# A spectral layer and a gated SwiGLU on one core: the D transform first, gate and up over both token groups, h times w2 in seven products, the sequence transform last

## The chip, the core and the metric

The kernel runs on one core of a Trainium2 chip. The metric is the time of one execution on the device, in microseconds (us); the median of three runs of the kernel before is 728.52 us (728.14 to 728.65). Engines in the text: TensorE (PE; its weight loads are PEld), VectorE (DVE), ScalarE (ACT), GpSimd (POOL, used here to start DMAs) and SyncE (SP, which starts most DMAs). On-chip memory is SBUF; matmul results go to PSUM, eight banks of 128 x 512 float32.

## The reference

For x of 2048 tokens by 512 features (S x D), in float32:

```
a = x @ hid_re.T ;  b = x @ hid_im.T            # transform along D
y = seq_re @ a - seq_im @ b                     # transform along S, real part
h = silu(x @ w1) * (x @ w3)                     # 1376 hidden features (F)
o = h @ w2
g = sigmoid((x * gate_w).sum(-1))
out = g * y + (1 - g) * o
```

## The kernel before

**Precision.** Each operand of a matmul is split into a high part, a copy rounded to the matmul's float32r format, and a low part, the difference (`split`, L75 to L77: a ScalarE copy, then a VectorE subtraction). `mm3` (L79 to L81) then issues three matmuls, high x high, high x low, low x high. So each product costs three 128x512 matmuls, and each operand one ACT and one DVE pass.

**Seven products.** A 2 x 2 block product is done with seven block products instead of eight (Strassen's scheme in Winograd's form). Sums of blocks of each operand are made first (the "forms" T1 to T4 on one side, `forms`, L95, on the other), and the seven results, P1 to P7, are added up out of PSUM. Gate and up, the sequence transform and the D transform are done this way; h times w2 is a plain product.

**Stages**, in this order:

1. Gate and up for token group 0 (1024 tokens). F is cut into 11 chunks of 128 (NC); w1 and w3 of a chunk and the two halves of D make the 2 x 2 blocks. The first chunk is done plainly, in eight products (`plain`, L340). `gate_up` (L308) runs over the others with `first1`, `first2` and `second`: 42 matmuls each. `prep_wa` and `prep_wb` make the weights' forms, three chunks ahead (LOOK). The gate score is the last column block of w1 (`put_score`).
2. `down` (L269) for group 0: h times w2, 264 matmuls into eight banks. The split w2 is also written to DRAM (`w2sp`).
3. Gate and up and `down` for group 1; w2 is read back from `w2sp`. Beside it `prep_d` (L110) makes the forms of the D matrices and writes them to DRAM (`dsp`), and `load_a` makes the forms of x for the sequence transform.
4. The sequence transform on x, four blocks of 512 transform rows (1344 matmuls `P<-zo,a`): `CHAIN` (L472) lists the seven products, `step` (L590) issues one of them, with four pieces (q) per product. `advance` (L534) runs ahead of it: loads eight steps ahead (`load_c`, LEAD + AHEAD), sums four ahead (`sum_c`), splits three ahead (`split_c`, L513). After the split of B22 a POOL DMA adds B12 to it in place (`accum_op`, L522). `spill` scales by the gate and writes to DRAM (`zsp`).
5. The D transform on these results, two blocks (336 matmuls `P<-zo,d`), reading `zsp`, then the closing sum with (1 - g) o from `nbsp`, and the output.

**What sets the order.** Each engine runs its instructions in the order of the built program; a scheduler lays that out beforehand from the dependencies, so it stays near the source order but not equal to it. The DMA queues of SP and POOL are in order too: a DMA that waits holds up those behind it. Most 4 KB-per-partition tiles come from one pool (`f4`, 13 buffers); a tile waits until the last user of its buffer is done, a store's landing included.

Of the kernel before, what the change touches and what calls it, by code (L numbers as in the profile page):

```python
# [12 lines left out]
P = 128  # L13
S = 2048
D = 512
F = 1376
KD = D // P
TB = 512
NTB = S // TB
NT = TB // P  # L20
NST = S // P
NG = NST // 2
NC = (F + P - 1) // P
NC2 = (NC + 1) // 2
WARM = 11
# [3 lines left out]
def fnet_swiglu_gate_kernel(  # L29
    ctx: ExitStack,  # L30
    tc: tile.TileContext,
    xn: bass.AP,
# [4 lines left out]
    w2: bass.AP,  # L37
    out: bass.AP,
# [6 lines left out]

    nc = tc.nc

    def pool(name, bufs, side, space=None):
        kw = {} if space is None else {"space": space}
        cm = tc.tile_pool(name=name, bufs=bufs, side=side, reuse_waits="tile", **kw)
        return cm, cm.__enter__()

    def close(*cms):
        for cm in reversed(cms):
            cm.__exit__(None, None, None)
# [4 lines left out]
    f4 = ctx.enter_context(tc.tile_pool(name="f4", bufs=13, side="right"))  # L63
    dn_cm, dn = pool("dn", 2, "right")
    xo_cm, xo = pool("xo", 1, "left")
    wo_cm, wo = pool("wo", 2, "left")
    tp_cm, tp = pool("tp", 2, "left")

    def bank(k, name):
        return psum.tile([P, 512], F32, tag=f"ps{k}", name=name)  # L70

    def wide(name):
        return f4.tile([P, 1024], F32, tag="f4", name=name)

    def split(hi, lo, src):  # L75
        nc.scalar.activation(hi, src, AF.Copy)  # L76
        nc.vector.tensor_sub(lo, src, hi.bitcast(F32))  # L77

# [4 lines left out]

    act0 = const.tile([P, 1], F32, tag="act0", name="act0")
    nbsp = dram.tile([D, S], F32, tag="nbsp", name="nbsp")
    gs = dram.tile([NTB, 1, 512], F32, tag="gs", name="gs")
    gsp = dram.tile([2, P, 1024], F32, tag="gsp", name="gsp")
    dsp = [dram.tile([KD, P, 2, n, 256], F32, tag=f"dsp{n}", name=f"dsp{n}") for n in (4, 3)]
    w2sp = dram.tile([NC, P, 2, 512], F32, tag="w2sp", name="w2sp")
    zsp = dram.tile([4 * NTB * P, 1024], F32, tag="zsp", name="zsp")  # L90

    def flat(ap):
        return ap.rearrange("p a n -> p (a n)")

    def forms(r, m, t1, t2):  # L95

        r, m = (v.rearrange("p (a n) -> p a n", a=4) for v in (r, m))
        a21, a11, a12, a22 = (r[:, i] for i in range(4))  # L100
        nc.vector.tensor_sub(m[:, 0], a22, a21)  # L101
        for d, v, w in ((1, m[:, 0], a11), (2, a12, m[:, 1])):
            nc.vector.scalar_tensor_tensor(m[:, d], v, -1.0, w, op0=ALU.mult, op1=ALU.subtract)  # L103
        nc.vector.tensor_sub(m[:, 3], a11, a21)  # L104
        split(t1[:, 0, 0], t1[:, 1, 0], a11)
        split(flat(t1[:, 0, 1:4]), flat(t1[:, 1, 1:4]), flat(m[:, 0:3]))
        split(flat(t2[:, 0, 0:2]), flat(t2[:, 1, 0:2]), flat(r[:, 2:4]))
        split(t2[:, 0, 2], t2[:, 1, 2], m[:, 3])

    def prep_d(p):  # L110

        r, m = wide(f"dr{p}"), wide(f"dm{p}")
        t1 = dn.tile([P, 2, 4, 256], F32R, tag="ho", name=f"d1_{p}")
        t2 = dn.tile([P, 2, 4, 256], F32R, tag="ho", name=f"d2_{p}")[:, :, :3]
        nc.sync.dma_start(r, dd[p])
        forms(r, m, t1, t2)
        nc.sync.dma_start(dsp[0][p], t1.bitcast(F32))
        nc.sync.dma_start(dsp[1][p], t2.bitcast(F32))


    XO, ST = {}, {}
    XRAW = ("B12", "B11", "B21", "B22")

    def flat_x(ap):
        return ap.rearrange("p q n -> p (q n)")

    def load_xo(g, k):

        if g not in XO:
            XO[g] = xo.tile([P, 2, 7, 2, 512], F32R, tag="xo", name=f"xo{g}")  # L130
        ST[g, k] = wide(f"xs{g}_{k}")
        nc.sync.dma_start(ST[g, k], xt[g, XRAW.index(k)])

    OPS = ("B11", "B21", "B22", "T1", "T2", "T3", "T4")
    SUMS = {"T1": ("B12", "B11"), "T2": ("B22", "T1"), "T3": ("B22", "B12"), "T4": ("B21", "T2")}

    def sum_xo(g, k):
        ST[g, k] = wide(f"xs{g}_{k}")
        nc.vector.tensor_sub(ST[g, k], *(ST[g, v] for v in SUMS[k]))

    def split_xo(g, k):
        o = XO[g][:, :, OPS.index(k)]
        split(flat_x(o[:, 0]), flat_x(o[:, 1]), ST[g, k])

    WS, WA, WB = {}, {}, {}
    LOOK = 3

    def load_w(i, lo=0, hi=4, queue=nc.sync):
        if lo == 0:
            WS[i] = wo.tile([P, 4, 256], F32, tag="ws", name=f"ws{i}", bufs=LOOK + 1)  # L150
        queue.dma_start(WS[i][:, lo:hi].rearrange("p a n -> p (a n)"),
                          w13[i % NC, :, lo * 256 : hi * 256])

    def prep_wa(i, lo=0, hi=3):

        if lo == 0:
            WA[i] = wo.tile([P, 2, 3, 256], F32R, tag="wa", name=f"wa{i}", bufs=LOOK + 1)
        t = WA[i]
        split(t[:, 0, lo:hi].rearrange("p a n -> p (a n)"),
              t[:, 1, lo:hi].rearrange("p a n -> p (a n)"),  # L160
              WS[i][:, lo:hi].rearrange("p a n -> p (a n)"))

    def prep_wb(i, part=None):

        if part != 1:
            w = WS.pop(i)
            u = wo.tile([P, 4, 256], F32, tag="wu", name=f"wu{i}", bufs=1)
            nc.vector.tensor_add(u[:, 0], w[:, 3], w[:, 2])
            nc.vector.tensor_sub(u[:, 1], u[:, 0], w[:, 0])
            nc.vector.tensor_sub(u[:, 2], w[:, 0], w[:, 3])  # L170
            nc.vector.tensor_sub(u[:, 3], w[:, 1], u[:, 1])
            WB[i] = u
        if part != 0:
            u = WB[i]
            t = wo.tile([P, 2, 4, 256], F32R, tag="wb", name=f"wb{i}")
            split(t[:, 0].rearrange("p a n -> p (a n)"), t[:, 1].rearrange("p a n -> p (a n)"),
                  u.rearrange("p a n -> p (a n)"))
            WB[i] = t

    def prod(ps, i, wi, xi, start, chain=False):  # L180
        g = i // NC
        w, wi = (WA[i], wi) if wi < 3 else (WB[i], wi - 3)
        x = XO[g]
        for q in range(2):
            sl = slice(q * P, (q + 1) * P)
            mm3(ps, w[:, 0, wi, sl], w[:, 1, wi, sl], x[:, 0, xi, q, :], x[:, 1, xi, q, :],
                start and q == 0, q == 1, chain)

    G, H = {}, {}

    def first1(i):
        x = bank(i % 4, f"X{i}")
        prod(x, i, 0, 0, True)
        s1 = tp.tile([P, 512], F32, tag="s1", name=f"s1_{i}", bufs=LOOK + 2)
        nc.scalar.activation(s1, x, AF.Copy)
        G[i] = (x, s1)

    def first2(i):

        y = bank(4 + i % 2, f"Y{i}")  # L200
        prod(y, i, 1, 1, True)
        s1 = G[i][1]
        nc.vector.tensor_add(s1, s1, y)
        put_score(i, 0, s1)
        nc.scalar.activation(s1, s1, AF.Silu)

    SC = {}

    def put_score(i, j, gate):


        if i % NC < NC - 1:
            return
        if j == 0:
            SC[i] = tp.tile([P, 2, 512], F32, tag="sc", name=f"sc{i}", bufs=1)
        nc.scalar.activation(SC[i][F % P :, j], gate[F % P :], AF.Copy)
        if j == 1:
            nc.sync.dma_start(gs[2 * (i // NC) : 2 * (i // NC) + 2].rearrange("b o n -> o b n"),
                              SC[i][F % P : F % P + 1])

    def second(i, between):
        x, s1 = G.pop(i)
        z = bank(6 + i % 2, f"Z{i}")
        u2 = tp.tile([P, 512], F32, tag="u2", name=f"u2_{i}")
        u4 = tp.tile([P, 512], F32, tag="u4", name=f"u4_{i}")
        g1 = tp.tile([P, 512], F32, tag="g1", name=f"g1_{i}")
        h = wide(f"h{i}")
        H[i] = h
        prod(x, i, 4, 4, False, True)
        nc.scalar.activation(u2, x, AF.Copy)  # L230
        prod(z, i, 5, 5, True, True)
        nc.scalar.activation(u4, z, AF.Copy)
        between[0]()
        prod(x, i, 3, 3, False, True)
        nc.vector.tensor_add(u4, u4, x)
        prod(z, i, 2, 6, False, True)
        nc.vector.tensor_add(u2, u2, z)
        nc.vector.tensor_mul(h[:, :512], s1, u2)
        between[1]()
        prod(x, i, 6, 2, False, True)  # L240
        put_score(i, 1, x)
        nc.scalar.activation(g1, x, AF.Silu)
        nc.vector.tensor_mul(h[:, 512:], g1, u4)

    HO, W2R, W2O = {}, {}, {}

    def load_w2(i):
# [21 lines left out]
    def down(g, extra):  # L269
# [4 lines left out]
        for c in range(NC):  # L274
            if c == 0:
                load_w2(g * NC + 1)
# [444 lines left out]
```

## Time and profile before

| | |
|---|---|
| median of three runs | 728.52 us |
| the profiled execution, first to last instruction (span) | 728.3 us |
| instructions | 8383 |
| matmuls | 3149, 11 of them warm-up |
| moved by DMA | 132.41 MB, 182 GB/s on average |
| mean granted TensorE clock | 0.996 |

The runs' times and the span differ by about 0.2 us, so a span can be read as a time. In the profile a line of a group gives the source line, engine, operation, output<-input, shape and count, then the busy time in us and the mean of one instruction in ns, then the idle time of that engine just before and what ended it. Because `split` and `mm3` are helpers, groups are told apart by their tiles.

### The profile page before, as it was taken

The page shows a single profiled execution, that of the slowest core. Times are in us where ns is not written, and L with a number is a line of the kernel's source. Part 1 is how long each engine was busy: PE and PEld are TensorE (multiplying, and loading weights), DVE is VectorE, ACT ScalarE, POOL GpSimd, SP SyncE. Part 2 cuts the span into 40 slices and gives each one's busy share as a digit, 9 for nine tenths or more (in the row PEclk, how much of TensorE's full clock was granted, in tenths as well). Part 3 has the DMA queues.
Part 4 walks back from the last instruction along what each step waited for, and adds up shares of the span by engine and source line. Part 5 has one row for each costly group of instructions (what it writes and reads, how often), then busy time and mean ns, then how long its engine had stood idle before and what let it go on. Part 6 is the DMA issues. An engine that isn't in the chain of part 4 may idle for free.

```text
span 728.3 us, 8383 instructions
## 1 busy us (share of the span) xinstructions
PE 720.7 (99%) x3149; PEld 590.7 (81%) x3149; DVE 542.9 (75%) x677; ACT 358.5 (49%) x458; POOL 21.3 (3%) x28
## 2 busy tenths in 40 slices
PE   9999999999999999998999999999999999999997
PEld 6888878888888888877888888888888888888886
DVE  6987786574598974799867786687758785667875
ACT  6655555454475743565444444444444444445451
POOL 0000000000000000000010001000000001000000
PEclk9999999999999999999999999999999999999999
DMA  6112135833157503585957733874195719999942
GB/s 259 59 58 87 58 118 200 291 128 145 37 188 279 191 1 99 182 328 196 377 95 240 257 120 64 243 246 155 29 234 185 253 23 218 366 380 305 332 161 86
DMA packets 37772, 132.41 MB, mean 182 GB/s; under 512 B 3938, under 2 KB 4322, under 8 KB 36708
## 3 DMA queue, kind: packets, MB, share of 16 engines
q1 hardware_dynamic: 33988, 118.90, 45.6%
q0 software_dynamic: 3456, 12.58, 9.5%
q8 instruction: 24, 0.39, 0.2%
q10 hardware_dynamic: 288, 0.39, 0.1%
q14 instruction: 16, 0.13, 0.1%
HBM read 100.93 MB, written 30.94 MB: 181 GB/s over the span
## 4 chain that ended last, share of the span: by engine, by line
PE 93%; DVE 3%; DMA 2%; ACT 1%; issue 1%; SPq 0%; DVEq 0%; ACTq 0%
PE P L81 52%; PE X L81 15%; PE acc L81 12%; PE Z L81 8%; PE Y L81 4%; PE C L81 2%; DVE a L77 1%; DMA w2o<-w2sp 1%; DMA xr<-xn 1%; DMA xs_B<-xt 1%; DVE xm L103 0%; DVE xm L101 0%; DVE xm L104 0%; ACT L303 0%; DVE ho L77 0%
## 5 line engine op out<-in xcount | busy, mean ns | idle before, releaser
L81 PE MATMUL P<-zo,a 128*128 128x512 f32 x1344 | 304.8, 389 | 0.0
L81 PEld LDWEIGHTS P<-zo,a 128*128 128x128 f32 x1344 | 252.3, 188 | 52.4
L76 ACT ACTIVATE zo<-B 128x1024 fp32r<-128x1024 f32 x124 | 131.4, 1060 | 159.9 <-PE P L81 148.4
L77 DVE TENSOR_TENSOR zo<-B,zo 128x1024 fp32r<-128x1024 f32 x124 | 151.5, 1223 | 76.5 <-ACT zo L76 76.1
L81 PE MATMUL acc<-ho,w2o 128*128 128x512 f32 x528 | 122.3, 393 | 2.4 <-DMA w2o<-w2sp 1.9
L81 PEld LDWEIGHTS acc<-ho,w2o 128*128 128x128 f32 x528 | 100.1, 190 | 24.3 <-ACT a L76 3.2
L81 PE MATMUL X<-xo,wb 128*128 128x512 f32 x378 | 94.2, 390 | 0.2
L81 PEld LDWEIGHTS X<-xo,wb 128*128 128x128 f32 x378 | 70.5, 188 | 16.3 <-ACT u L230 0.6
L81 PE MATMUL P<-zo,d 128*128 128x512 f32 x336 | 76.3, 389 | 0.0
L81 PEld LDWEIGHTS P<-zo,d 128*128 128x128 f32 x336 | 63.1, 188 | 13.1
L511 DVE TENSOR_TENSOR B<-B,B 128x1024 f32<-128x1024 f32 x48 | 58.5, 1224 | 6.5 <-DMA B<-cc 2.7
L77 DVE TENSOR_TENSOR ho<-h,ho 128x1024 fp32r<-128x1024 f32 x22 | 26.9, 1222 | 9.7 <-ACT ho L76 9.7
L81 PE MATMUL X<-xo,wa 128*128 128x512 f32 x126 | 33.1, 391 | 0.0
L81 PE MATMUL Z<-xo,wb 128*128 128x512 f32 x126 | 32.3, 389 | 0.0
L77 DVE TENSOR_TENSOR wb<-wu,wb 128x1024 fp32r<-128x1024 f32 x21 | 25.7, 1224 | 8.6 <-ACT wb L76 8.3
L81 PE MATMUL Y<-xo,wa 128*128 128x512 f32 x126 | 32.1, 389 | 0.0
L76 ACT ACTIVATE wa<-ws 128x768 fp32r<-128x768 f32 (+2 forms) x23 | 18.8, 817 | 27.0 <-PE Z L81 25.5
L81 PE MATMUL Z<-xo,wa 128*128 128x512 f32 x126 | 32.0, 389 | 0.0
L522 POOL DMA_DIRECT2D B<-cc x16 | 14.1, 879 | 546.1 <-DVE zo L77 546.1
L77 DVE TENSOR_TENSOR zo<-T,zo 128x1024 fp32r<-128x1024 f32 x16 | 19.6, 1223 | 12.4 <-ACT zo L76 12.4
L81 PEld LDWEIGHTS X<-xo,wa 128*128 128x128 f32 x126 | 23.5, 188 | 5.4 <-DVE wa L77 0.6
L81 PEld LDWEIGHTS Z<-xo,wa 128*128 128x128 f32 x126 | 23.6, 188 | 5.0
(95 smaller groups left out, 594.4 us busy)
## 6 DMA issues: line engine op xcount, KB each, us to landing
B<-cc SPq DMA_DIRECT2D x64, 512.0 KB, 4.7
ws<-w SPq DMA_DIRECT2D x21, 512.0 KB, 3.7
B<-cc POOLq DMA_DIRECT2D x16, 512.0 KB, 5.5
B<-zsp SPq DMA_DIRECT2D x12, 512.0 KB, 11.1
w2sp<-w2o SPq DMA_DIRECT2D x11, 512.0 KB, 2.8
w2o<-w2sp SPq DMA_DIRECT2D x11, 512.0 KB, 5.4
xs_B<-xt SPq DMA_DIRECT2D x8, 512.0 KB, 5.4
nbsp<-b SPq DMA_DIRECT2D x8, 512.0 KB, 3.3
```

What stands on the lines that cost most here:

```text
L76: nc.scalar.activation(hi, src, AF.Copy)
L77: nc.vector.tensor_sub(lo, src, hi.bitcast(F32))
L81: nc.tensor.matmul(ps, u, v, start=first and n == 0, stop=last and n == 2, skip_group_check=chain)
L511: nc.vector.tensor_add(t, t, RAW[blk, b, q])
L522: nc.gpsimd.dma_start(src, block(blk, "B12", q), accum_op=ALU.add)
```

## The change

- **Order of stages.** The D transform is done first, on x (`hidden`, two token groups), and its results a and b go to DRAM (`ab`). Gate and up follow, then h times w2, then the sequence transform on a and b, which ends in the output.
- **Gate and up** run over both token groups for each of the 11 chunks (`item`, 84 matmuls per chunk, tiles of 128 x 1024 over two banks). h goes to DRAM (`hsp`, and `hpl` for the last chunk).
- **h times w2** is done in seven products over ten chunks, in the same loop as the sequence transform (`BLOCKS`: w2, a and b, two token halves each); the last chunk is added plainly ("pl" steps).
- **Forms kept in DRAM.** The forms of w2, of a and of part of b are made during gate and up (`forms`, `later`, `work`), split, written to DRAM (`fsp`) and read back (`load_a`) when their block comes; three forms of b are made in its first block.
- **Queues.** The stores of `ab`, `hsp`, `fsp`, `nbsp` and `ysp` are issued from POOL; before, all but the accumulating DMAs were issued from SP or ACT.
- **Pools.** One `f4` pool of 19 buffers, a pool of 28 for x's forms and later for the forms read back, and 8 half buffers for the split moving operands. Nine warm-up matmuls instead of 11.

The diff, cut to its core:

```diff
+    f4 = ctx.enter_context(tc.tile_pool(name="f4", bufs=19, side="right"))
+    zo = ctx.enter_context(tc.tile_pool(name="zo", bufs=8, side="left"))
+    op = ctx.enter_context(tc.tile_pool(name="op", bufs=28, side="left"))
...
+    DORD = (("P1", "B11", "B11"), ("P2", "B21", "B21"), ("P5", "F3", "v5"), ("P6", "F2", "v6"),
+            ("P7", "F1", "v7"), ("P3", "F4", "B22"), ("P4", "B22", "v4"))
+
+    def store_ab(g, c, n, j, t):
+        nc.gpsimd.dma_start(ab[c, g, 2 * n + j].rearrange("p h i e -> p (h i e)"), t)
...
+    def store_h(c, n, t):
+        o = hpl[:, n] if c == NC - 1 else hsp[:, c // NP, n, c % NP]
+        nc.gpsimd.dma_start(o.rearrange("g p n -> p g n"), half(t))
+
+    def item(c, hooks):
+        x, s1, wa, wb = X[c], S1[c], WA[c], WB[c]
+        z = pair(3, f"Z{c}")
+        u2, u4, g1 = raw(f"u2_{c}"), raw(f"u4_{c}"), None
+        prod(x, wb, 1, "F2", False)
+        nc.scalar.activation(u2, flat(x), AF.Copy)
+        prod(z, wb, 2, "F3", True)
+        nc.scalar.activation(u4, flat(z), AF.Copy)
+        hooks[0]()
+        if c + 1 < NC:
+            first1(c + 1)
+        hooks[1]()
+        prod(x, wb, 0, "F1", False)
+        nc.vector.tensor_add(u4, u4, flat(x))
+        hooks[2]()
+        prod(z, wa, 2, "F4", False)
+        nc.vector.tensor_add(u2, u2, flat(z))
+        nc.vector.tensor_mul(u2, u2, s1)
+        store_h(c, 0, u2)
+        hooks[3]()
+        if c + 1 < NC:
+            first2(c + 1)
+        hooks[4]()
+        prod(x, wb, 3, "B22", False)
...
+            pool, tag = (op, "op") if keep else (f4, "f4")
+            t = pool.tile([P, 2, n], F32R, tag=tag, name=f"f{m}{k}{q}")
+            split(t[:, 0], t[:, 1], src)
+            if keep:
+                A[m, k, q] = t
+            else:
+                nc.gpsimd.dma_start(fsp[m, PRODS.index(k), q, :, : 2 * n], flat(t.bitcast(F32)))
...
+    BLOCKS = [(m, j) for m in range(3) for j in range(G)]
+    CHAIN = (("P1", "B11"), ("P5", "F1"), ("P6", "F2"), ("P3", "B22"),
+             ("P7", "F3"), ("P2", "B21"), ("P4", "F4"))
...
+        for r in range(2):
+            for c in (slice(0, 256), slice(256, 512)) if r else (slice(0, 512),):
+                nc.vector.tensor_mul(t[:, r, c], ps[:, r, c], half(GT[b])[:, n, c])
+                nc.vector.tensor_sub(t[:, r, c], half(o[0])[:, r, c], t[:, r, c])
+                (nc.scalar if c.start == 0 and r else nc.sync).dma_start(rows[:, r, c], t[:, r, c])
...
+    later = []
+    for q in range(NQS[0]):
+        later += forms(0, q, PRODS, False)
+    later += prep_w2l()
+    for q in range(NQ):
+        later += forms(2, q, PRODS, False)
+    for q in range(NQ):
+        later += forms(1, q, ("P1", "P5", "P6", "P3"), False)
+    per = -(-len(later) // ((NC - 1) * 5))
```

More of the change, by code (lines that the diff above doesn't have):

```diff
@@ L180, in prod @@
[L180 to L196, printed above, removed]
@@ new lines, in prod, with first1 @@
+    def prod(ps, w, k, xk, start, chain=True):
+        for g in range(G):
+            xh, xl = XF[g, xk]
+            for q in range(2):
+                sl = slice(q * P, (q + 1) * P)
+                mm3(ps[:, g], w[0][:, k, sl], w[1][:, k, sl], xh[:, q], xl[:, q],
+                    start and q == 0, q == 1, chain)
+    X, S1 = {}, {}
+    def first1(c):
+        X[c] = pair(c % 2, f"X{c}")
+        prod(X[c], WA[c], 0, "B11", True)
+        S1[c] = raw(f"s1_{c}")
+        nc.scalar.activation(S1[c], flat(X[c]), AF.Copy)
@@ new lines, in fnet_swiglu_gate_kernel, with block, chunks, load_c @@
+    LEAD, AHEAD = 3, 5
+    RAW, ZO, PL = {}, {}, {}
+    def block(b, k, q):
+        m, j = BLOCKS[b]
+        if m == 0:
+            v = hsp[j, int(k[1]) - 1, int(k[2]) - 1, 2 * q : min(2 * q + 2, NP)]
+            return v.rearrange("c p n -> p c n")
+        return half(cc[m - 1, j, ("B11", "B12", "B22", "B21").index(k), q])
+    def chunks(b, q):
+        return width(BLOCKS[b][0], q) // 256
+    def load_c(n):
+        while LOADS and LOADS[0][0] <= n:
+            _, b, k, q = LOADS.pop(0)
+            w = chunks(b, q)
+            r = RAW[b, k, q] = raw(f"{k}_{b}_{q}", w * 512)
+            nc.sync.dma_start(half(r, w), block(b, k, q))
@@ new lines, in sum_c, with split_c @@
+    def sum_c(n):
+        if not 0 <= n < len(STEPS):
+            return
+        b, k, q, form = STEPS[n]
+        o = {"F1": "B11", "F2": "B22", "F4": "B21"}.get(form)
+        if o and q != "pl":
+            t = RAW[b, "B12", q]
+            nc.vector.tensor_add(t, t, RAW[b, o, q])
+    def split_c(n):
+        if not 0 <= n < len(STEPS):
+            return
+        b, k, q, form = STEPS[n]
+        if q == "pl":
+            r = PL[b]
+            if form == "n1" and k == "P3":
+                t = zo.tile([P, 1024], F32R, tag="zo", name=f"zp{n}")
+                split(t[:, :512], t[:, 512:], r["n1"])
+                r["z"] = t
+            elif form == "n1":
+                ZO[n] = r["z"][:, :512], r["z"][:, 512:]
+                return
+            else:
+                if form == "n01":
+                    nc.vector.tensor_sub(r["n0"], r["n0"], r["n1"])
+                t = zo.tile([P, 1024], F32R, tag="zo", name=f"zp{n}")
+                split(t[:, :512], t[:, 512:], r["n0"])
+            ZO[n] = t[:, :512], t[:, 512:]
+            return
+        w = chunks(b, q) * 512
+        src = RAW[b, {"F1": "B12", "F2": "B12", "F4": "B12", "F3": "B22"}.get(form, form), q]
+        h, l = (zo.tile([P, w], F32R, tag="zo", name=f"z{v}{n}") for v in "hl")
+        split(h, l, src)
+        ZO[n] = h, l
+        if form == "B22":
+            nc.gpsimd.dma_start(half(src, chunks(b, q)), block(b, "B12", q), accum_op=ALU.add)
@@ new lines, in fnet_swiglu_gate_kernel, with run @@
+    LASTS = []
+    def run(*gens):
+        for gen in gens:
+            for _ in gen:
+                pass
+    xg, dg = load_x(0, "B11", 2), load_d("B11", 2)
+    for _ in range(2):
+        next(xg)
+        next(dg)
+    warm = f4.tile([P, 512], mybir.dt.bfloat16, tag="f4", name="warm")
+    nc.vector.memset(warm, 0.0)
+    wps = pair(3, "wps")
+    for n in range(WARM):
+        nc.tensor.matmul(wps[:, 0], warm[:, :P], warm, start=True, stop=True)
+    nc.scalar.activation(act0, warm[:, :1], AF.Silu)
@@ new lines, in fx, with fd @@
+    def fx(g, n):
+        if n < len(DORD):
+            form_x(g, DORD[n][1])
+    def fd(n):
+        if n < len(DORD):
+            form_d(DORD[n][2])
+    hooks = {n: [lambda n=n: fx(0, n + 2), lambda n=n: fd(n + 2)] for n in range(5)}
+    for n, k in enumerate(("B11", "B21", "B12", "B22")):
+        hooks[n + 2 if n < 3 else 4].append(lambda k=k: run(load_x(1, k)))
+    hooks[5] = [lambda: fx(1, 0)]
+    hooks[6] = [lambda: fx(1, 1)]
+    hidden(0, hooks)
+    hooks = {n: [lambda n=n: fx(1, n + 2)] for n in range(5)}
@@ new lines, in fnet_swiglu_gate_kernel, with work, h0, h1 @@
+    per = -(-len(later) // ((NC - 1) * 5))
+    def work(count):
+        for _ in range(count):
+            if later:
+                later.pop(0)()
+    for c in range(NC):
+        def h0(c=c):
+            if c + 2 < NC:
+                load_w(c + 2)
+            work(per)
+        def h1(c=c):
+            if c + 1 < NC:
+                prep_wb(c + 1)
+            work(per - 1)
+        def h2(c=c):
+            work(per)
+            if c == NC - 1:
+                load_a(0, "P1")
+                load_c(3)
+        def h3(c=c):
+            work(per)
+            if c == NC - 1:
+                load_a(0, "P5")
+                advance(-4)
+                advance(-3)
+        def h4(c=c):
+            if c + 2 < NC:
+                prep_wa(c + 2)
+            work(per)
+            if c == NC - 1:
+                advance(-2)
+                advance(-1)
+        item(c, (h0, h1, h2, h3, h4))
@@ L667 @@
+    for b in range(2, 6):
+        act(b, "P1", lambda b=b: load_gate(b))
+    start = AT[2, "P1", 0]
+    for q in range(NQ):
+        for i, f in enumerate(forms(1, q, ("P7", "P2", "P4"), True)):
+            TASKS.setdefault(start + 3 * q + max(i - 1, 0), []).append(f)
+    for i, k in enumerate(ks):
+        act(3 if i < 6 else 4, ks[(i + 1) % 7], lambda k=k: load_a(2, k))
+    for n in range(len(STEPS)):
+        step(n)
 def kernel(**inputs):
```

884 lines of the change are left out of this document (377 added, 507 removed).

## The prediction

> **What bounds the kernel now.** I read the page first, then the cores, the chain of work that ended last, the stretches, and the groups by form.
>
> ```profile
> span 728.3 us, 8383 instructions
> PE 720.7 (99%) x3149; PEld 590.7 (81%) x3149; DVE 542.9 (75%) x677; ACT 358.5 (49%) x458; POOL 21.3 (3%) x28
> PE 93%; DVE 3%; DMA 2%; ACT 1%; issue 1%; SPq 0%; DVEq 0%; ACTq 0%
> q1 hardware_dynamic: 33988, 118.90, 45.6%
> q0 software_dynamic: 3456, 12.58, 9.5%
> ```
>
> TensorE is busy all the time and is 93% of the chain. The chain in order of time gives the price of one matmul:
>
> ```profile
> 5.87 0.70 DVE xo L77
> 6.62 8.99 PE C L81 x37
> ...
> 343.68 380.82 PE P L81 x1680
> ```
>
> In the last stretch nothing but TensorE is on the chain: 380.82 / 1680 = 226.7 ns for a 128x512 matmul. There are 3149 − 11 warm-up = 3138 of them, so 711.3 us at that pace. The other 17.0 us: the last stretch ends at 343.68 + 380.82 = 724.5, so 3.8 us are the tail; before 343.68 stand 1458 matmuls (330.5 us), so 13.2 us were lost there. About 5.9 of these are the wait for the first data, and 3.4 lie between 312 and 344:
>
> ```profile
> 6.00:12.00 6.00, 5.95 (x25) 1.00 1.02 415
> ...
> 312.00:324.00 12.00, 11.56 (x51) 1.00 0.89 342
> ...
> 332.00:337.00 5.00, 3.13 (x14) 1.00 0.85 322
> 337.00:344.00 7.00, 7.00 (x26) 0.76 0.04 15
> ...
> PE acc L81 <- DMA w2o<-w2sp: 1.9, 1, 1.9
> ```
>
> (Columns: stretch, length, PE busy, granted clock, DMA share, GB/s; the last row is a wait: total, times, longest.) PE idled 0.4 and 1.9 us, the latter for a reloaded w2 form, and behind that the clock fell to 0.76: 26 matmuls in 7 us are 269 ns each, so a stall costs more than itself, about 26 × (269 − 227) ns = 1.1 us. The remaining 3.9 us go mostly in the first 30 us. The span of the profiled execution is 728.3 us, the median of the timed runs 728.52; I work against the span and add the 0.2.
>
> **What the change does to TensorE.** Counted from the instruction order of the built program, all 128x512: transform along D 2 × 7 × 24 = 336; gate/up 11 × 84 = 924; h times w2 2 × (7 × 30 + 4 × 6) = 468; sequence transform 4 × 7 × 48 = 1344. Sum 3072, which is 66 fewer (528 → 468 from the seven products, 930 → 924 since the first chunk is no longer eight products). At 226.7 ns: **696.4 us**, a gain of 15.0. Everything else is what may take it back.
>
> **Head.** The first DMAs are two halves of 256 KB instead of 128 + 512 KB, so the first matmul starts near 6.1 us. But the whole D form set is now needed at once: VectorE has 4 operations of 512 and 18 of 1024 elements before the low half that the fifth product (P7) waits for.
>
> ```profile
> L77 DVE TENSOR_TENSOR zo<-B,zo 128x1024 fp32r<-128x1024 f32 x124 | 151.5, 1223 | 76.5 <-ACT zo L76 76.1
> L77 DVE TENSOR_TENSOR wa<-ws,wa 128x768 fp32r<-128x768 f32 x21 | 20.0, 951 | 0.0
> L235 DVE TENSOR_TENSOR u<-u,X 128x512 f32<-128x512 f32 x21 | 14.4, 685 | 14.6 <-PE X L81 14.5
> L168 DVE TENSOR_TENSOR wu<-ws 128x256 f32<-128x256 f32 x21 | 8.8, 420 | 0.3
> L76 ACT ACTIVATE zo<-B 128x1024 fp32r<-128x1024 f32 x124 | 131.4, 1060 | 159.9 <-PE P L81 148.4 <-issue 4.9 <-DMA B<-zsp 1.7
> ```
>
> 4 × 0.685 + 18 × 1.223 = 24.8 us from 5.9, plus about 1 us where the queue stands for data and for the first result: 31.7. TensorE alone would be there at 6.1 + 96 × 0.2267 = 27.9. So 3.8 us are lost to VectorE and the head costs 6.1 + 3.8 = 9.9 us, as much as before (5.9 + 3.9). It could be 0.9 better with no waits. Behind P7 VectorE has room (20 operations per 38 us).
>
> **Gate/up.** One chunk now holds 84 matmuls, 19.04 us. VectorE per chunk: split of wa 0.951, forms of wb 4 × 0.420 + 1.223, five operations of 1024 (two PSUM sums, s1 + y, two products) 6.1: 10.0 us. Into nine chunks go all the forms of w2, a and b: per group 7 splits and 4 sums of 512, 7.5 us, 69 us together. From the order of the built program, between the gate sums of chunk 1 and of chunk 8, it comes to 124.4 us for 7 chunks: **17.8 of 19.04, 93%**. ScalarE has 11.5. Is 93% too much? Two stretches of before bear on it (columns: length, then PE, PEld, DVE, ACT, POOL busy, clock, DMA, GB/s):
>
> ```profile
> 10.00:40.00 30.00, 30.00 (x131) 24.36 (x131) 29.18 (x40) 21.23 (x29) 0.00 (x0) 1.00 0.25 92
> 200.00:250.00 50.00, 50.00 (x221) 41.02 (x220) 46.43 (x86) 33.28 (x54) 0.00 (x0) 1.00 0.66 236
> 600.00:700.00 100.00, 100.00 (x443) 82.81 (x442) 69.97 (x69) 46.27 (x51) 9.17 (x11) 1.00 0.98 316
> ```
>
> DVE at 97% and at 93%, and PE full both times. A sum out of PSUM has two products (5.4 us) before TensorE needs its bank, so a late VectorE has room. But new waits stand in its queue and in ScalarE's: the form tiles share 19 buffers with everything else, and an operation that takes one waits until an old store has landed; behind it wait the PSUM sums, and for these TensorE. Stores: ten of 524 KB per chunk and three loads, 6.8 MB in 19.04 us = **358 GB/s**. The page's hardware queue moved 118.90 MB in 45.6% of 728.3 us = 358 GB/s while busy, and where it was pressed, 415 (row above). Stores alone:
>
> ```profile
> 207.00:208.00 1.00, 1.00 (x6) 0.81 (x5) 1.00 (x3) 0.00 (x0) 0.00 (x0) 1.00 1.02 399
> 208.00:209.00 1.00, 1.00 (x6) 0.84 (x5) 1.00 (x3) 0.85 (x1) 0.00 (x0) 1.00 1.15 463
> ```
>
> (the 1.75 MB of one D form going out), 400 and more. So the demand fits, with 10 to 15% left. I put 3 us here; the bounds are 0 and, if the DMA held only the 322 of the quoted row, (6.8 / 0.322 − 19.04) × 7 = 14.5.
>
> **The queues the stores move to.** The stores go from SP to POOL, 24 issues become 146.
>
> ```profile
> L522 POOL DMA_DIRECT2D B<-cc x16: 862/866/1007, 371.7 to 608.1; - x16
> B<-cc POOLq DMA_DIRECT2D x16, 512.0 KB, 5.5
> w2sp<-w2o SPq DMA_DIRECT2D x11, 512.0 KB, 2.8
> ```
>
> (First row: min/median/max ns.) Ten issues of 0.87 take 8.7 of 19.04 us; the queue is in order, but the schedule lays them out in the order of their producers.
>
> **Changes of stage.** From D to gate/up the weight forms are made beside the second D group. Into h times w2: the first forms reload when the x forms are freed, the raw h loads stand behind them on SP and go out after the last chunk's first product, 10.9 us ahead of use. The low parts fall between 1 and 3 us before TensorE wants them. 2 us for both; 0 to 3.4 (what before lost between 312 and 344).
>
> **h times w2 and the sequence.** VectorE has 43 of 53 us in a w2 block, 62 to 67 of 76.2 in a sequence block (28 splits, 12 sums, 3 PSUM sums, up to 12 closing ones of 1.22). That is 82 to 88%; the row of 600 to 700 has 70%, with PE full. The DMA is fullest in the second sequence block of the first half: 48 plain transfers (25.2 MB) and 4 accumulating ones. The software queue shows 9.5% of 728.3 us / 24 = 2.88 us each, so at 415 GB/s 72 us of 76, at 358 82 us. What lags has a whole block of time, as it did in 600 to 700 above. 1 us; 0 to 5.6.
>
> **Tail.** Before ended so:
>
> ```profile
> 724.53 0.76 DVE L572 TENSOR_TENSOR zc<-P,nb 128x256 f32<-128x256 f32 x2 [1.72 <-PE P L81]
> ```
>
> Now each last quarter is a product and a difference, so two more 256-element operations, 0.84: 3.8 → 4.6.
>
> **Sum.** 696.4 + 9.9 + 3 + 2 + 1 + 4.6 = 716.9; with 0.2 **717 us**, 1.6% less.
>
> **Rivals.**
> *The forecast*: TensorE keeps its pace, 710 to 722. For it: the two DVE rows and the DMA rows.
> *Gate/up gives it back through buffer waits*: VectorE has 1.2 us of room per chunk. Its waits for ScalarE averaged 1.07 us:
>
> ```profile
> DVE zo L77 <- ACT zo L76: 88.5, 83, 2.0
> ```
>
> If three such waits per chunk come where TensorE cannot wait, 3.2 − 1.2 = 2.0 us × 9 = 18 on 714, so 728 with the clock's price inside the spread, 720 to 736. Against it: the 5.4 us that TensorE allows, since a VectorE that runs late meets fewer waits.
> *Slower: the POOL queue's transfers are slow in themselves.* The only price of that queue in the trace is 12.58 MB in 69.2 us, 182 GB/s. If that is the queue and not the accumulation (which moves the data twice), the 43.3 MB of gate/up stores take 238 us where about 9.3 chunks, 177 us, are to be had: 61 us more, **775 us**. It turns slower than before as soon as these stores run below 43.3 / 191.5 = 226 GB/s. The Trainium skill (DMA: Bandwidth & Descriptors, section Measured (HBM→SBUF, 128 partitions, SWDGE, issued from GpSimd)) has 6.15 us for a plain 1 MB on that path, 341 GB/s; by it 43.3 MB would be 127 us and would fit. No run here shows a plain transfer on it yet.
> *VectorE holds up POOL's issues*: if each of them first waited for one operation of 1.22, an issue would be 2.09 us and ten of them 20.9, 1.9 × 7 = 13 us more: 730. The sixteen issues at 862 to 1007 ns, beside a DVE that was 75% busy over the span, speak against it. The Trainium skill (SBUF — State Buffer, section SBUF: two separate sides) warns of just this for stores moved to GpSimd, but names VectorE's two-port fast modes as the cause; the long operations here run at 1223 ns, the only fast one is this, and it occurs twice:
>
> ```profile
> L304 DVE TENSOR_SCALAR ng<-gt 128x1024 f32<-128x1024 f32 x2 | 1.4, 694 | 4.4 <-ACT gt L303 4.4
> ```
>
> *The sequence runs short of DMA*: the 5.6 above and a clock price or two, 719 to 726, centre 723.
> That the matmuls do not become fewer is no rival: the built program has 3081 with 9 for warm-up.
>
> **Chances.** Forecast 0.57; buffer waits 0.22 (faster 0.11, same 0.03, slower 0.08); slow POOL transfers 0.08; held issues 0.04 (same 0.01, slower 0.03); short sequence 0.09 (faster 0.07, same 0.01, slower 0.01). A measurement of this kernel tells 0.2% from no change, 727.1 to 730.0. Faster 0.75, same 0.05, slower 0.20. The range 710 to 738 holds the forecast, the buffer waits and the sequence case; only the slow queue and part of the rest lie outside.
>
> **What would show it.** PE's matmul count 3081 and its pace 226.7 ns in the sequence stretch; first P7 matmuls of the D stage near 32 us; gate/up chunks 19.0 us apart (21 or more: buffer waits, with DVE and ACT waiting for DMA; 25 or more: the queue); POOL issues at 0.87; stores landing in 3 to 8 us; DMA share above 0.9 in gate/up at 340 to 400 GB/s. If the DMA share is 1.0 there at under 250 GB/s, the forecast is wrong by its queue; if it is low while PE idles, by its buffers or its order.

## The result and the profile after

| | before | after |
|---|---|---|
| median | 728.42 us (728.14 to 728.65, four runs) | **740.3 us** (739.72 to 742.51, four runs) |
| the profiled execution: time, span | 728.3 us span | 739.72 us, 737.9 us span |
| mean granted clock | 0.996 | 0.986 |
| matmuls | 3149 | 3081 |

The ratio is 1.0165, with a 95% interval of 1.0149 to 1.0181: **slower by 1.65%**, where 1.6% faster was forecast; 740.3 lies above the range of 710 to 738. (Between a run's time and its span stood 1.8 us for after, and as much for before in all its later runs; so spans are compared with spans here.)

The page of after, the span and the busy times:

```profile
span 737.9 us, 8598 instructions
PE 711.0 (96%) x3081; PEld 580.5 (79%) x3081; DVE 541.5 (73%) x579; ACT 337.7 (46%) x380; POOL 92.2 (12%) x150
```

The 68 fewer matmuls are there, but TensorE is busy for 711.0 us where 3072 × 226.7 ns would be 696.4, and idle for 26.9 us. Where that is, TensorE's busy time by stretches of 30 us around the two blocks of h times w2 shows (columns: stretch, length, PE busy and matmuls, granted clock, DMA share, GB/s):

```profile
290.00:320.00 30.00, 28.95 (x125) 1.00 0.95 354
320.00:350.00 30.00, 23.37 (x85) 0.83 0.98 306
350.00:380.00 30.00, 30.00 (x134) 1.00 0.80 289
380.00:410.00 30.00, 23.81 (x96) 0.89 1.00 323
410.00:440.00 30.00, 30.00 (x134) 1.00 0.80 271
```

A full stretch holds 134 matmuls. Two stretches hold 85 and 96, and the granted clock falls in both. The first and last matmul of these blocks, and the first of the next stage (min/median/max ns of one, then the start of the first and of the last):

```profile
L71 PE MATMUL P<-zh,a0P x280: 387/389/796, 295.9 to 422.2; 128*128 128x512 f32 x140
...
L71 PE MATMUL P<-zh,a1P x256: 389/389/389, 423.8 to 543.3; 128*128 128x512 f32 x128
```

From 295.9 to 423.8 are 127.9 us for 468 matmuls that need 106.1: **21.8 us lost** in these blocks, about as much as the whole miss (a span of 737.9 where 716.9 was forecast, 21.0). Who waits for whom there, from the waits between 295 and 425 (total, times, longest), and one case of it on ScalarE:

```profile
ACT zh L63 <- DMA B<-hsp: 34.0, 8, 9.6
PEld P L71 <- ACT zh L63: 12.7, 4, 6.1
PE P L71 <- ACT zh L63: 11.1, 3, 5.7
...
336.33 1.06 ACT L63 ACTIVATE zh<-B 128x1024 fp32r<-128x1024 f32 x1 [8.44 <-DMA B<-hsp]
```

TensorE waits for a split on ScalarE, and ScalarE for a transfer from `hsp`, the stored h. Most of that is not for a plain load: 27.8 of the 34.0 us, six times, are waits for the six transfers of `split_c` (L419), where a POOL DMA adds B12 onto B22 in SBUF to make F3 for the product P7. POOL's instructions there in the first block, and the median times from issue to landing:

```profile
316.35 1.24 POOL L419 DMA_DIRECT2D B<-hsp  x1 [8.93 <-DVE zl L64]
327.08 2.14 POOL L419 DMA_DIRECT2D B<-hsp  x2 [9.50 <-issue]
...
B<-cc POOLq DMA_DIRECT2D x16, 512.0 KB, 6.2
...
B<-hsp POOLq DMA_DIRECT2D x4, 512.0 KB, 9.7
B<-hsp POOLq DMA_DIRECT2D x2, 256.0 KB, 11.3
```

Two things show. The second of three goes out 10.7 us after the first: POOL idled 9.5 us between them, and the releaser is "issue", so it waited for nothing that the profile shows. It went on just as the first transfer had landed (that one took 10.4 us, 316.35 + 10.4 = 326.75). In the second block the second goes out 9.2 us after the first (378.59, then 387.81); there the profile names a load of a form as the releaser, but the first had landed just then too (8.9 us). And one by one the six take 8.9 to 12.2 us to land, where the median from `cc` is 6.2. The time between issue and need is fixed by the loop: the P7 split of a piece stands three pieces of P3 and one plain step behind it, (12 + 12 + 6 + 6) matmuls × 0.2267 = 8.2 us; in the sequence stage it is 4 × 12 × 0.2267 = 10.9 us. So a transfer of 6.2 us fits and one of 9.7 doesn't, and three of them in single file even less.

### The profile page after: what moved, and what is told of

Its sections match the earlier page's. It is cut to its first block, busy times and chain, and to the rows that moved or that the text cites. A ratio compares the mean times of both kernels' runs of the same rounds, so it can differ in the third digit from the quotient of the medians.

```text
span 737.9 us, 8598 instructions
## 1 busy us (share of the span) xinstructions
PE 711.0 (96%) x3081; PEld 580.5 (79%) x3081; DVE 541.5 (73%) x579; ACT 337.7 (46%) x380; POOL 92.2 (12%) x150
## 4 chain that ended last, share of the span: by engine, by line
PE 70%; issue 15%; DMA 7%; DVE 3%; POOL 3%; ACT 1%; SPq 1%; POOLq 0%; ACTq 0%; DVEq 0%
PE P L71 48%; PE X L71 8%; PE dX L71 5%; PE Z L71 4%; DMA B<-hsp 3%; PE dZ1P L71 2%; PE Y L71 2%; DMA B<-cc 2%; POOL fsp L337 2%; DMA xB<-xt 1%; POOL hsp L251 1%; PE dZ0P L71 1%; DMA a1P<-fsp 1%; DVE zl L64 1%; ACT zh L63 0%
## 5 line engine op out<-in xcount | busy, mean ns | idle before, releaser
L63 ACT ACTIVATE zh<-B 128x1024 fp32r<-128x1024 f32 x154 | 156.5, 1021 | 236.1 <-PE P L71 169.5
L64 DVE TENSOR_TENSOR zl<-B,zh 128x1024 fp32r<-128x1024 f32 x154 | 179.1, 1172 | 92.3 <-ACT zh L63 91.8
L71 PE MATMUL P<-zh,a2P 128*128 128x512 f32 x448 | 138.1, 389 | 0.0
L71 PE MATMUL P<-zh,a0P 128*128 128x512 f32 x280 | 92.1, 405 | 11.1 <-ACT zh L63 11.1
L71 PEld LDWEIGHTS P<-zh,a2P 128*128 128x128 f32 x448 | 84.1, 188 | 17.6
L71 PE MATMUL P<-zl,a2P 128*128 128x512 f32 x224 | 87.1, 389 | 0.0
L391 DVE TENSOR_TENSOR B<-B,B 128x1024 f32<-128x1024 f32 (+1 forms) x66 | 76.9, 1170 | 10.7 <-DMA B<-cc 7.5
L71 PE MATMUL P<-zh,a1P 128*128 128x512 f32 x256 | 79.2, 389 | 0.0
L71 PE MATMUL P<-zl,a0P 128*128 128x512 f32 x140 | 57.4, 410 | 2.7 <-DVE zl L64 2.7
L71 PE MATMUL P<-zh,f1P 128*128 128x512 f32 x192 | 59.5, 389 | 0.0
L419 POOL DMA_DIRECT2D B<-cc x16 | 13.8, 861 | 155.3 <-DVE zl L64 153.0
L244 DVE TENSOR_TENSOR s<-s,Y 128x1024 f32<-128x1024 f32 x11 | 13.4, 1215 | 11.8 <-PE Y L71 10.1
```

The lines of the kernel that those rows point to most:

```text
L71: nc.tensor.matmul(ps, u, v, start=first and n == 0, stop=last and n == 2, skip_group_check=chain)
L244: nc.vector.tensor_add(S1[c], S1[c], flat(y))
L391: nc.vector.tensor_add(t, t, RAW[b, o, q])
L419: nc.gpsimd.dma_start(half(src, chunks(b, q)), block(b, "B12", q), accum_op=ALU.add)
```

## The experiments

Three theories for those 21.8 us. **A**: the buffer for POOL's descriptors (the entries that tell the DMA engines what to move) holds one such transfer at a time. **B**: the transfers are cut up badly (2 KB rows). **C**: they land late because the DMA engines are full just then (share 0.98 to 1.0), as the forms and h are all read back at once. Times are of one run unless an interval is given; before took 728.72 us in the first set (e1 to e3) and 731.57 in the second (e4 to e6), so a difference of 3 us between the sets says nothing.

**e1_ring.** The buffer that holds the descriptors of POOL's transfers is doubled.

```
-    ... num_devices=1, dynamic_dma_scratch_size=1024)
+    ... num_devices=1, dynamic_dma_scratch_size=2048)
```

> Only the ring that POOL's software queue writes its descriptors to is doubled (1024 to 2048). In the changed kernel the first accumulating DMA of each h times w2 block lands 9 to 10.5 us after its issue, and the second is issued only then (316.35, then 327.08; 378.59, then 387.81). Theory ring (two of them do not fit the ring): the second goes out within 2 us of the first, the stalls of 4.5 and 5.7 us and most of the slow clock behind them go, 740 falls to 727 to 731. Theory pressure (the DMA engines are full there, so anything lands late, and the second issue waits for something else): no change, 738 to 741. Theory rows (rows of 2 KB make an accumulating DMA slow in itself): the second goes out early, but lands no earlier than 18 to 20 us after the first was issued; 736 to 740.

Measured: 732.61 us, span 730.8. POOL's line, and the two stretches:

```profile
317.15 3.41 POOL L419 DMA_DIRECT2D B<-hsp  x3 [9.06 <-DVE zl L64]
...
320.00:350.00 30.00, 25.46 (x108) 1.00 1.06 351
...
380.00:410.00 30.00, 26.82 (x112) 0.94 1.04 368
...
B<-hsp POOLq DMA_DIRECT2D x4, 512.0 KB, 10.6
B<-hsp POOLq DMA_DIRECT2D x2, 256.0 KB, 12.8
```

The three go out back to back in 3.41 us, and in the second block POOL waits only for VectorE between them: A is shown for the held issue. But they land after 10.6 and 12.8 us (medians), no faster. The blocks run from 296.7 to 415.8, 119.1 us: A is worth **8.8 us** of the 21.8, and 11 us more have another cause.

**e2_rows.** `hsp` is laid out so that a row holds two chunks, 4 KB, which makes half as many rows; the buffer stays at 1024.

```
-    hsp = dram.tile([G, 2, 2, NP, P, 512], ...)
+    hsp = dram.tile([G, 2, 2, (NP + 1) // 2, P, 2, 512], ...)
```

> h of two chunks is laid side by side in DRAM, so that an h load or an accumulating DMA of two chunks has 128 rows of 4 KB instead of 256 of 2 KB; its stores keep 2 KB rows. Theory rows: the accumulating DMAs of h land in about 6.2 us like those of the sequence matrices, the stalls go, 740 falls to 718 to 722. Theory ring: half the descriptors per DMA, so that two fit: the second is issued within 2 us; the first still lands near 9; 725 to 731. Theory pressure: landing stays at 9 to 10 and the time at 737 to 741.

Measured: 732.17 us, span 730.4. The issues stand at 317.09, 318.20 and 319.40, so with half the rows the old buffer is enough; landing takes 9.4 and 11.7 us (medians), and the blocks 296.7 to 416.3, 119.6 us. The rows explain the held issue (two transfers of 256 rows do not go out together, two of 128 do) and not the late landing: B falls for the rest.

**e3_noacc.** In the two blocks of h times w2 the accumulating DMA is left out; VectorE makes F3 as F2 − B11 from what is in SBUF.

```
+        if form == "B22" and BLOCKS[b][0] == 0:
+            nc.vector.tensor_sub(src, RAW[b, "B12", q], RAW[b, "B11", q])
-        if form == "B22":
+        elif form == "B22":
             nc.gpsimd.dma_start(..., accum_op=ALU.add)
```

> In the two h times w2 blocks VectorE forms B12 + B22 as (B12 + B11 + B22) - B11, both already in SBUF, and the six accumulating DMAs are gone; five operations of 1024 or 512 more per pair of blocks on VectorE, 3.1 us per block, and B11's buffers are held one product longer. All three theories of the accumulating DMA: both blocks run near 53 us each, 740 falls to 718 to 722, and TensorE's granted clock stays at 1.0 from 320 to 410. Rival (raw h loads and form reloads come late too, and the next one of them takes the stall's place): above 728.

Measured: **721.06 us**, span 719.3.

```profile
320.00:350.00 30.00, 30.00 (x134) 1.00 1.00 388
...
380.00:410.00 30.00, 30.00 (x134) 1.00 0.99 383
```

TensorE is full, at clock 1.00, though the DMA share is still 0.99 to 1.00 and the plain transfers land no faster. The blocks take 297.1 to 405.2, 108.1 us. So 19.8 of the 21.8 us hang on those six transfers of L419, and with them gone the change is faster than before. Timed again as **e9_noacc_t**:

> The kernel of e3_noacc, timed in rounds against the kernel before. If the two blocks of h times w2 hold all that the prediction had left out, the ratio to before is 0.989 to 0.990 as in the one look (721.06 over 728.72) with an interval that lies below 1; if that look was lucky, it is above 0.992.

Measured: 720.99 us (720.4 to 722.3, four runs) against 728.78 (728.38 to 730.24, seven runs), ratio 0.9894, interval 0.9879 to 0.9908. The gain of the single run was not luck.

**e4_fewloads.** The accumulating transfers stay, in e2's layout, but the DMA engines are relieved: of the forms read back in `load_a` for w2 and for the first sequence blocks only P1's are loaded and all seven products use them, so the right values of h times w2 and of half the sequence transform are left out.

```
         for q in range(NQS[m]):
+            if m < 2 and k != "P1":
+                A[m, k, q] = A[m, "P1", q]
+                continue
```

> Leaves out: in stage w2 and in the first sequence blocks (m = 0 and 1) only the forms of P1 are read back, and all seven products use them, so the output is not the reference's. The accumulating transfers of F3 stay, in the layout of e2_rows (which took 732.2 us, accumulating transfers landing 9.4 and 11.7 us). Theory A (they land late because the DMA engines are full, share 0.94 to 1.04 there): with 18 of 36 loads gone from the two h times w2 blocks they land in 6 to 7 us as those from cc did (6.2), the two blocks take 106 to 110 us instead of 119.6, and the run 720 to 723 us. Theory B (accumulating onto what was just written in DRAM, or from 256 rows, is slow in itself): landing stays 9 to 12 us, the blocks about 118 to 120, the run 731 to 733.

Measured: 716.94 us, span 715.1.

```profile
320.00:350.00 30.00, 29.36 (x127) 1.00 0.72 231
...
380.00:410.00 30.00, 30.00 (x134) 1.00 0.81 277
...
B<-hsp POOLq DMA_DIRECT2D x4, 512.0 KB, 7.8
B<-hsp POOLq DMA_DIRECT2D x2, 256.0 KB, 8.5
```

The blocks take 296.8 to 404.5, 107.7 us, as with no such transfer at all: with the reloads gone, the 11 us are gone, and C is supported. (The DMA share in the two pressed stretches was 1.03 to 1.04 in e2 and is 0.72 to 0.81 here; the 0.94 in the expectation is the clock's column, misread.) The medians of 7.8 and 8.5 hide how it came about, since the two blocks differ:

- In the first block the transfers land no faster, after 10.1 to 11.0 us (9.4 to 13.1 in e2). The DMA share there, from 310 to 325, is still 0.99 to 1.05. But the first goes out at 313.2 instead of 317.1, since the splits ahead of it are earlier too, and TensorE loses only 0.6 us from 320 to 350.
- In the second block they land after 5.4 to 6.1 us instead of 6.8 to 10.2, at a mean share of 0.72 from 365 to 380.

So it was an earlier start in one block and a faster landing in the other. Fewer loads also leave SP's queue shorter, and what that alone is worth was not tested.

That landing follows the load on the DMA engines, and not the source of the data, can be read in the trace of after itself. The median of 6.2 us for transfers from `cc`, all cut up alike, covers four blocks that differ:

| four transfers from `cc`, stretch | DMA share | GB/s | landing, median |
|---|---|---|---|
| 450 to 470 | 0.98 | 248 | 10.1 us |
| 527 to 546 | 0.97 | 247 | 9.4 us |
| 606 to 625 | 0.79 | 178 | 5.2 us |
| 682 to 701 | 0.69 | 138 | 5.2 us |

The four transfers themselves are 105 to 110 of these GB/s (2.1 MB in 19 or 20 us). So 137 to 143 GB/s of other traffic ran beside them in the first two rows, and 28 to 68 in the last two.

**e5_spforms.** e3 with the 65 stores of the forms issued from SP again, as a test of the rival of the POOL queue.

```
-                nc.gpsimd.dma_start(fsp[m, PRODS.index(k), ...
+                nc.sync.dma_start(fsp[m, PRODS.index(k), ...
```

> e3_noacc (721.1 us) with the 65 stores of the forms on SyncE's queue instead of GpSimd's. Theory A (GpSimd's queue is not what costs; the 10 us of the head and the waits behind full DMA engines are): the run stays within 2 us of 721, and if the 1.8 us between the run and its span come from the number of software transfers (150 instructions), they shrink to about 1.1 us. Rival (the queue of the stores costs gate/up or what follows): the run falls by 3 us or more. A loss of 3 us or more says that stores on SyncE hold up the loads behind them.

Measured: 742.9 us, span 741.1. The waits of SP's queue between 90 and 300 us, and TensorE from 90 to 310, where e3 is full (200.00 of 200 from 90 to 290):

```profile
SPq L337 <- DVE f2P L64: 45.8, 20, 6.7
SPq L337 <- DVE wu L67: 41.0, 7, 26.4
...
90.00:310.00 220.00, 205.37 (x879) 0.98 0.78 282
```

A store on SP waits for its producer on VectorE, with the loads of the next chunk queued behind it. ScalarE then waits 10.9 us for late loads from `ab`, VectorE 8.6 us for one of the weights, and TensorE 10.1 us for ScalarE's `g`; in e3 these three come to 0.5 us together. That the one leads to the other is read from the waits. The first matmul of h times w2 starts at 318.6 instead of e3's 297.1, so 21.5 us are lost, 14.6 of them as TensorE's idle time in the row above. So putting the form stores on the POOL queue, which I had feared, is worth some 21 us in the change's favour. The 1.8 us outside the span stay (742.9 − 741.1), so they aren't the number of POOL's transfers.

**e6_spread.** e3 with two edits against what was left: the reads of `a2` go out one at a time, two steps behind the release of their buffers, and the last product's first half is finished ahead of the second half's matmuls.

```
-        act(3 if i < 6 else 4, ks[(i + 1) % 7], lambda k=k: load_a(2, k))
+        for q in range(NQ):
+            TASKS.setdefault(AT[3, k, q] + 2, []).append(lambda k=k, q=q: load_a(2, k, [q]))
...
             for r in range(2):
+                if r and n == len(STEPS) - 1:
+                    last_part(b, *QUARTER[k], end, ps, 0)   # product, difference, store of r = 0
```

> e3_noacc (721.1 us) with two edits: the reads of the third group's forms (a2) go out one by one, two steps after the buffers that they take are free, instead of four at each product's start, where SyncE waited up to 19 us for TensorE with the loads of cc queued behind; and the last product's first half is finished before the second half's matmuls are issued. Theory (the 2.8 us lost at 530 to 560 us are SyncE's order, and 1.3 us of the tail is the wait for the last matmul of both halves): TensorE has 30 of 30 us in 530 to 560, the tail falls from 5.9 to 4.6 us, the run takes 716.5 to 718 us. Rival (the DMA engines are simply short of time in that stage): the 2.8 us stay, 719 to 720 us.

Measured: 721.27 us, span 719.5, where e3 had 719.3: nothing gained. The tail did what was expected: the last matmul ends at 714.9 and the span at 719.5, 4.6 us instead of 5.9. The spreading did not, and the sequence took 2.1 us longer from its first matmul to its last (310.3 us, e3 308.2):

```profile
510.00:520.00 10.00, 10.00 (x46) 8.29 (x45) 3.93 (x4) 4.10 (x4) 2.55 (x3) 1.00 1.01 248
520.00:530.00 10.00, 10.00 (x45) 8.05 (x43) 2.39 (x2) 4.25 (x4) 0.00 (x0) 1.00 1.05 329
530.00:540.00 10.00, 7.58 (x27) 6.00 (x27) 9.95 (x10) 2.63 (x3) 0.36 (x1) 0.83 1.03 412
```

(Columns: PE, PEld, DVE, ACT, POOL busy, clock, share, GB/s.) The DMA engines are full from 510 on, but at 248 GB/s, while POOL issues its accumulating transfers; at the same share 412 were moved once these were through. TensorE is short there as it was in e3 (7.18 of 10 us from 530 to 540), so the theory of SP's order falls. The new one: these transfers use up the engines' time.

**e7_block3.** e3, the edit of the tail, and the subtraction also in the fourth block (m = 1, second group), the one that runs then.

```
-        if form == "B22" and BLOCKS[b][0] == 0:
+        if form == "B22" and b in (0, 1, 3):
```

> e3_noacc (721.1 us) with the four accumulating transfers of the fourth block (m = 1, second group) replaced by four more subtractions on VectorE, and the last product's first half finished before the second half's matmuls. Theory (accumulating transfers fill the DMA engines at 510 to 520 us: share 1.01 at 248 GB/s, where plain ones reach 413 GB/s at the same share, so the loads of cc land late): TensorE has 29 to 30 of 30 us in 530 to 560 instead of 27.2, and with 1.3 us from the tail the run takes 716.5 to 718 us. Rival (the bytes alone are too many there, since four loads of a form, four of cc and one more take 9 transfers of 512 KB per 11 us): 27 to 28 of 30 stay, 719 to 720 us.

Measured: **717.02 us** (716.53 to 717.75, four runs), span 714.9, ratio 0.984, interval 0.9823 to 0.9856.

```profile
510.00:520.00 10.00, 10.00 (x46) 8.29 (x45) 7.69 (x7) 5.17 (x5) 0.00 (x0) 1.00 0.69 260
520.00:530.00 10.00, 10.00 (x46) 8.29 (x45) 9.95 (x9) 3.80 (x4) 0.00 (x0) 1.00 1.02 412
530.00:540.00 10.00, 10.00 (x46) 8.28 (x45) 9.54 (x10) 3.65 (x4) 0.54 (x1) 1.00 0.90 314
```

With four transfers gone, more is moved from 510 to 520 (260 GB/s, e3 247) at a share of 0.69 instead of 1.01, and TensorE is full. The sequence takes 305.9 us instead of the 308.2 and 308.9 of the two profiles of e3's kernel; the tail gives the other 1.3. **e8_allsub** does so in all six blocks (`if form == "B22":`).

> As e7_block3, but with no accumulating transfer at all: all six blocks form F3 by a subtraction on VectorE (16 more of 1.2 us than e3_noacc). Theory (they cost nothing where VectorE has room, 76% busy): 716 to 718 us, as e7_block3 or 0 to 1 us below. Rival (B11 is held two products longer, so the loads into the 19 buffers of f4 come later, or VectorE, full from 540 to 580 us, becomes late): TensorE loses 3 to 10 us in the sequence stage, 720 to 727 us.

Measured: 717.8 us (716.18 to 719.04, four runs), ratio 0.9846, interval 0.9827 to 0.9865. The two intervals overlap: no further gain shows, and no loss. Both versions are faster than before and after.

## Why the prediction was wrong

**The step that failed: "h times w2 and the sequence".** There I asked whether VectorE and the DMA engines had enough time per block, and put 1 us on it; in the two blocks of h times w2 alone 21.8 us were lost, 19.8 of them by the six accumulating transfers of L419 (e3). I did not ask what each product waits for: the accumulating DMA, which before ran only in the two transforms, now also made F3 in h times w2. Its landing time stood in the prediction as 5.5 us, quoted under POOL's issues and set against no window; into the sum of this step only its 2.88 us of the DMA engines' time went. The list of before had a second row for that queue, which I passed over:

```profile
B<-cc POOLq DMA_DIRECT2D x16, 512.0 KB, 5.5
...
T<-zsp POOLq DMA_DIRECT2D x8, 512.0 KB, 10.4
```

The trace of before splits these by load as that of after does: the `cc` transfers landed after 5.4 to 6.8 us at DMA shares of 0.59 to 0.66 (medians of four), the one of `zsp` at 0.51 after 5.3, and the other seven, at 0.93 to 1.04, after 8.7 to 11.4 (medians of one or two). So against a window of 8.2 us, which can be counted from the loop, 10.4 us would have shown ScalarE waiting in each block of w2. TensorE is three steps behind it, and how much of the wait reaches it, the 11 us, the trace of before does not give. I also did not count how many of these transfers come in a row with rows of 2 KB. The trace of before shows no held issue, so that part, 8.8 us, could not be read from it at all.

Point by point, span against span:

| step | forecast, us lost | measured |
|---|---|---|
| matmuls, count and pace | 3072 × 226.7 ns | 3081 with 9 for warm-up; 227.1 ns in the last stretch of the chain (176.88 / 779) |
| head, gate/up, changes of stage | 9.9 + 3 + 2 = 14.9 | 10.3 up to 295.9 |
| h times w2 | none of its own | 21.8 |
| sequence | 1 | 3.5 |
| tail | 4.6 | 5.9 |

The sum of the differences is −4.6 + 21.8 + 2.5 + 1.3 = 21.0 us, and 737.9 − 716.9 is 21.0 too. That the loss in h times w2 is about as large as the whole miss is chance: the other differences nearly cancel.

- **Head and pace: right.** The chain of after has the P7 matmuls of the D stage where 31.7 was forecast, and TensorE alone at its end:

```profile
31.48 5.81 PE dX L71 x24
...
555.16 176.88 PE P L71 x779
```

- **Gate/up: better than forecast.** TensorE was full from 90 to 290, even in the stretch from 220 to 230 with VectorE at 97% and the DMA share at 1.02. Over the whole the share was 0.84 at 312 GB/s, less than the 0.9 at 340 to 400 that I had expected:

```profile
220.00:230.00 10.00, 10.00 (x46) 8.29 (x45) 9.71 (x13) 5.34 (x7) 2.88 (x5) 1.00 1.02 389
90.00:290.00 200.00, 200.00 (x885) 1.00 0.84 312
```

  The rival of buffer waits did not come. (Its sum was wrong too: 18 us on 714 are 732 and not 728.)
- **The POOL queue: both rivals refuted.** The stores of the forms and of h land in 4.7 to 6.2 us (medians), and an issue takes 0.54 to 0.72 us, less than the 0.87 that I had taken from the accumulating ones:

```profile
fsp<-f2P POOLq DMA_DIRECT2D x28, 512.0 KB, 6.2
hsp<-u POOLq DMA_DIRECT2D x20, 512.0 KB, 6.0
...
L337 POOL DMA_DIRECT2D fsp<-f2P x28 | 15.2, 542 | 41.8 <-DVE f2P L64 37.0 <-ACT f2P L63 2.6 <-DVE wu L67 1.1
```

  The doubt that I had voiced, that 182 GB/s is the accumulation and not the queue, was the right reading for these stores; I used it only to defend the stores, and not against the accumulating transfers that stayed. Of the held issues by VectorE, of which the Trainium skill (SBUF — State Buffer, section SBUF: two separate sides) warns, nothing shows at 542 ns, with VectorE at 91% where these 28 were issued. As the prediction noted, that warning is for VectorE's two-port fast modes, of which it found only two operations, so this row does not test it. The two figures that the prediction quoted beside the rival of slow transfers, 6.15 us for 1 MB and 341 GB/s, do not go together (1 MB in 6.15 us is 170 GB/s); at 170 the stores would not have fitted, so what speaks for them is the trace of after.
- **The price of a stall was too small.** I had 1.1 us for the slow clock behind a stall. Here one wait came after the other (TensorE alone from 325 to 350, in stretches of 5 us):

```profile
325.00:330.00 5.00, 2.87 (x10) 0.89 1.06 383
330.00:335.00 5.00, 3.41 (x11) 0.77 1.09 302
335.00:340.00 5.00, 2.09 (x4) 0.57 0.89 265
340.00:345.00 5.00, 5.00 (x18) 0.75 0.78 239
345.00:350.00 5.00, 5.00 (x24) 1.00 1.01 352
```

  Of the 21.8 us TensorE's recorded waits make 13.8 (11.1 for ScalarE, 2.7 for VectorE); of the other 8.0, 6.1 are matmuls that took longer in the two stretches with clocks of 0.83 and 0.89 ((23.37 − 85 × 0.2267) + (23.81 − 96 × 0.2267)), the slowest 796 ns instead of 389. The Trainium skill (TensorE: Matmul & The Clock Gate, section Part 1: The HAM clock gate) has the clock at half after an idle window of about 3.4 us; a matmul of twice the length, behind waits of up to 5.7 us, agrees.
- **"The sequence runs short of DMA": right, as a rival.** 3.5 us were lost, 2.8 of them at 540 to 560 in after. In e7, with the four accumulating transfers ahead of it replaced, TensorE is full there, so the loss hung on these and not on the plain loads alone.
- **The tail**: 1.3 us too small. I took the first half's product to follow its own matmuls; in after it waits for the last matmul of both halves, and two operations of 512 more stand behind the end. e6 shows that finishing the first half earlier brings the tail to the 4.6 forecast.

```profile
732.06 1.02 DVE L513 TENSOR_TENSOR uP<-P,gate 128x512 f32<-128x512 f32 x2 [6.13 <-PE P L71]
```

With ten accumulating transfers replaced by subtractions and the tail as I had assumed it (e7), the kernel takes the 717 us that were forecast for the change itself. The count of matmuls and their pace held; that the number agrees is partly luck. In span e7 is 2.0 us below the forecast of 716.9, since less was lost up to h times w2 than I had put there, and about 1.8 us instead of 0.2 lie outside the span. And it is a result of another kernel; the change as made has the wait, and the forecast for it was wrong.

## What to carry to other kernels

Before asking whether an engine has enough time in a stage, ask for each operand what its last producer is, how long that takes *under the load of this stage*, and how many matmuls stand between its issue and its use; a transfer that fitted a window of 10.9 us need not fit one of 8.2. When the profile has two rows for one kind of transfer, or a median over several stages, split it by stage and price with the stretch that is as full as the one in question. An accumulating DMA is no free addition: here one VectorE operation of 1.2 us on data that were in SBUF anyway did the same, off the path.

## What the runs showed of the hardware

- Whether POOL's queue issued a second accumulating transfer before the first had landed hung on rows and buffer: with 256 rows of 2 KB and a buffer of 1024 POOL idled 9.5 and 8.0 us ahead of the second, with 2048 or with 128 rows of 4 KB it did not.
- Accumulating transfers fill the DMA engines: with four of them beside plain loads 247 GB/s were moved at a share of 1.01 (e3, 510 to 520); without them 260 at 0.69, and 412 at 1.02 (e7).
- An accumulating transfer of 512 KB from `cc` landed in 5.2 us at DMA shares of 0.69 and 0.79 and in 9.4 to 10.1 at 0.97 to 0.98 (medians of four), in one execution (after).
- Plain stores from POOL, 43 MB of them in gate/up, cost 0.54 to 0.72 us each to issue and landed in 4.7 to 6.2 us (medians); with the form stores among them on SP the kernel took 21.8 us longer (span 741.1 instead of 719.3, e5 and e3).
